# Two attention-and-MLP layers on one core: low halves and b2 sums that go to GpSimd or VectorE as the plan finds room, and unit 1's residual on ScalarE

## The chip, the cores and the metric

The kernel runs on one core of one Trainium2 chip. The metric is device time in microseconds. Three runs of the kernel before gave 1146.32, 1146.71 and 1148.91, with a median of 1146.71.

## What is computed

The input x has 2048 rows of 640 numbers. The reference runs two layers; each one is an attention block and then an MLP block, with the same weights in both layers.

```
x = x + attention(layernorm(x), wqkv) @ wo
x = x + gelu(layernorm(x) @ w1 + b1) @ w2 + b2      # w1: 640 x 1536
# and the same two lines once more
```

The attention has 32 heads of 20 numbers. A query looks at eight keys: its own row and the rows 2, 4, ... 14 before it. So a logit is a sum over 20 products, and there are eight of them for a query and a head. The result is compared in float32 accuracy, which is why every matrix operand is split: a high half in float16 and a low half, the float16 of what the high half left out. A product of two split operands takes three matmuls (high by high, high by low, low by high).

## The kernel before: units, groups and a plan

The even and the odd rows are each cut into two sets of 512 (the attention reaches back in steps of two), and a set in one layer is a *unit*: units 0 to 3 are layer 1, units 4 to 7 are layer 2. A unit has four tiles of 128 rows. For a unit n the work is this.

- `layernorm` makes the normalised rows, the high half on ScalarE (line 615) and the low half on VectorE (line 617); a DMA transposes both for the next matmul.
- `qkv` multiplies by wqkv on TensorE (line 874; in units 5 to 7 a form with seven products instead of eight, line 802, whose extra sums and low halves are in `sums_of_rows`, lines 643 to 678). The result goes to DRAM and comes back by query and key (DMAs `qk`, `v`).
- `attention` runs on VectorE, once for each of four groups of eight heads: G = 4n to 4n+3. It multiplies queries by keys (line 965, 5120 elements a partition), sums over the 20 head dimensions (line 970, a reduction of the same 5120 elements), does the softmax on small tiles (lines 974 to 984, the exponential on ScalarE), multiplies by the values (line 986) and adds the eight keys up (lines 991 and 994). Line 999 takes the high half on ScalarE and line 1002 the low half.
- `project` multiplies by wo on TensorE (line 1027) after a transposing DMA (line 1015) of all four groups' halves. The residual is added in one of two ways. In seven units ScalarE first puts x into the PSUM bank (line 1039), the matmuls add to it, and ScalarE copies the sum back (line 1044). In unit 1 (`filled = n != 1`) VectorE adds bank and x instead (line 1036, two instructions of 320 elements a tile, eight in all).
- `mlp` goes over twelve slabs of 128 hidden columns. For each one TensorE makes the hidden values (line 1094, fifteen matmuls), ScalarE applies gelu and takes the high half (lines 1100, 1103), VectorE takes the low half (line 1105), and TensorE multiplies by w2 into five PSUM banks (line 1115; 24 matmuls a slab, the last third of which reads the low half). Units 6 and 7 of the MLP are done together at the end by `pair` and `joint` (lines 1170 to 1420), in a scheme with fewer products.
- b2 is added to x by GpSimd (line 624), once a tile.

No order is written by hand. Each step is handed to a `Plan` with an engine, a duration, a priority, the things it needs and the buffers it holds. `Plan.run` plays the program through once on the host, engine by engine, takes for each engine the ready step that can start first (with the priority to decide between near ones), and the instructions are then issued in the order of their planned starts. So the table of durations and priorities sets the order on every engine, and a change in one rule moves instructions everywhere.

GpSimd has a rule of its own. VectorE's steps with two operands in SBUF are marked as a pair (`PAIRS`), and a step on GpSimd marked so is not planned to start inside one of them; if it takes over 1 us in the plan, it also waits on the chip for the VectorE instruction that stands before it in the plan (`behind`), and VectorE's next pair step is planned after its end. Two kinds use this: the low half of the first three attention groups of a unit (line 1002, `ol` in the plan, planned at 1.7 us) and the sums with b2 (line 624, `xb`). The fourth group's low half is on VectorE.

## Time and profile before

| | us |
|---|---|
| median of three runs | 1146.71 |
| the profiled execution, whole | 1149.85 |
| its span, first to last instruction | 1148.1 |
| TensorE (PE) busy | 1125.1 |
| VectorE (DVE) busy | 1072.3 |
| ScalarE (ACT) busy | 630.2 |
| GpSimd (POOL) busy | 144.4 |
| mean granted TensorE clock | 0.999 |

The profiled execution is 1.75 us longer than its span, which holds what lies before the first and after the last instruction, and 3.14 us longer than the median. Lines of the profile give an engine, the source line, what is written and read, and how often. A matmul's duration in the profile reaches into the next one, so its cost is taken as a group's busy time over its count. PEclk is the clock that TensorE was granted, as a share of full speed.

### The profile page before, as it was taken

How to read it: one execution, taken by the hardware profiler on the slowest of the kernel's cores; microseconds unless marked ns; L12 is line 12 of the kernel's file. 1: busy time of each engine (PE TensorE's matmuls, PEld its weight loads, DVE VectorE, ACT ScalarE, POOL GpSimd, SP SyncE). 2: the span in 40 equal slices, each digit the busy share in tenths (PEclk: the TensorE clock that was granted, in tenths of full speed). 3: DMA queues.
4: the chain of work that ended last, by engine and by line, in shares of the span. 5: the costliest groups of instructions: out<-in, count | busy, mean ns of one | idle time of the engine just before them, and what ended most of it. 6: DMA issues, size and time to landing. Idle time of an engine off the chain costs nothing.

```text
span 1148.1 us, 16909 instructions
## 1 busy us (share of the span) xinstructions
PE 1125.1 (98%) x6560; PEld 604.1 (53%) x6560; DVE 1072.3 (93%) x901; ACT 630.2 (55%) x1163; POOL 144.4 (13%) x94
## 2 busy tenths in 40 slices
PE   9999999999999999999999999999999999989998
PEld 6444445445544465455555464456444655544476
DVE  7999999999999999999999999999999999498972
ACT  6367327343863373555567664388634852776630
POOL 1012014100041101100021002111220120010000
PEclk9999999999999999999999999999999999999999
DMA  9998784768787799568956879768878574896101
GB/s 320 304 299 256 206 197 143 206 219 252 219 279 199 219 283 285 190 240 213 323 163 217 196 220 298 226 195 185 231 252 242 215 192 139 215 219 178 45 24 69
DMA packets 257564, 246.05 MB, mean 214 GB/s; under 512 B 150524, under 2 KB 215116, under 8 KB 257484
## 3 DMA queue, kind: packets, MB, share of 16 engines
q1 hardware_dynamic: 257484, 244.98, 73.9%
q8 instruction: 51, 0.84, 0.3%
q14 instruction: 29, 0.24, 0.1%
HBM read 157.55 MB, written 52.64 MB: 183 GB/s over the span
## 4 chain that ended last, share of the span: by engine, by line
PE 32%; DVE 19%; issue 6%; ACT 5%; DMA 2%; POOL 1%; POOLq 0%; SPq 0%; DVEq 0%; ACTq 0%
PE ps L1094 8%; PE acc L1115 8%; PE ps L802 6%; PE ps L1027 4%; DVE pr L965 3%; PE acc L1296 3%; DVE sm L970 3%; DVE pr L991 2%; PE ps L1296 2%; DVE pr L986 2%; DVE pr L1228 2%; PE ps L1331 1%; DVE wq L736 1%; DMA wq<-ws0T 1%; DVE act L1105 1%
## 5 line engine op out<-in xcount | busy, mean ns | idle before, releaser
L1115 PE MATMUL acc<-c,act 128*128 128x512 f16 (+1 forms) x1728 | 249.0, 299 | 3.6 <-DVE xf L1159 2.0
L874 PE MATMUL ps<-wq,yT 128*128 128x480 f16 (+1 forms) x1230 | 244.4, 361 | 0.4 <-DVE yT L536 0.2
L1094 PE MATMUL ps<-yT,c 128*128 128x512 f16 x1080 | 243.1, 379 | 1.0 <-DMA yT<-w 1.0
L1115 PEld LDWEIGHTS <-act 128*128 128x128 f16 x1728 | 136.2, 98 | 113.2 <-issue 3.3
L874 PEld LDWEIGHTS <-yT 128*128 128x128 f16 x1230 | 118.9, 98 | 124.6 <-ACT yT L534 0.5
L965 DVE TENSOR_TENSOR pr<-qk 128x5120 f32<-128x5120 f32 x32 | 176.6, 5519 | 1.0 <-DMA qk<-spill 0.7
L986 DVE TENSOR_TENSOR pr<-sm,v 128x5120 f32<-128x5120 f32 x32 | 176.5, 5516 | 0.4
L970 DVE TENSOR_REDUCE sm<-pr 128x256 f32<-128x5120 f32 x32 | 175.1, 5472 | 0.1
L1094 PEld LDWEIGHTS <-c 128*128 128x128 f16 x1080 | 103.6, 98 | 122.2 <-issue 1.1
L991 DVE TENSOR_TENSOR pr<-pr 128x2560 f32<-128x2560 f32 x64 | 142.0, 2219 | 0.4
L1027 PE MATMUL ps<-wo,yT 128*128 128x320 f16 x960 | 134.4, 301 | 4.4 <-DMA yT<-ohl 2.6
L1027 PEld LDWEIGHTS <-yT 128*128 128x128 f16 x960 | 94.2, 98 | 43.7 <-DMA yT<-ohl 3.6
L1100 ACT ACTIVATE act<-ps,b 128x512 f32<-128x512 f32 x72 | 49.1, 682 | 106.2 <-PE ps L1094 105.5
L584 POOL TENSOR_TENSOR ln<-ln,half 128x2 f32<-128x2 f32 (+1 forms) x31 | 48.7, 1574 | 410.7 <-ACT ln L581 410.7
L1002 POOL TENSOR_TENSOR ohl<-w,ohl 128x640 f16<-128x640 f32 x24 | 49.2, 2049 | 401.1 <-DVE pr L965 202.2
L892 ACT ACTIVATE ev<-ps 128x480 f32<-128x480 f32 x80 | 45.1, 567 | 99.1 <-PE ps L874 94.9
L802 PE MATMUL ps<-wq,yT 128*128 128x480 f16 x396 | 84.3, 366 | 0.0
L811 ACT ACTIVATE ev<-ps 128x480 f32<-128x480 f32 x72 | 39.5, 565 | 49.3 <-PE ps L802 44.6
L802 PEld LDWEIGHTS <-yT 128*128 128x128 f16 x396 | 38.2, 98 | 40.0
L802 PE MATMUL ps<-wq 128*128 128x480 f16 x252 | 53.8, 366 | 2.9 <-ACT ev L811 2.1
L567 ACT ACTIVATE junk<-xf 128x640 f16<-128x640 f32 x57 | 41.7, 731 | 19.4 <-DVE xf L1036 11.7
L1105 DVE TENSOR_TENSOR act<-act 128x512 f16<-128x512 f32 x72 | 51.0, 716 | 1.0 <-ACT act L1103 0.8
(218 smaller groups left out, 1247.3 us busy)
## 6 DMA issues: line engine op xcount, KB each, us to landing
c<-mw SPq DMA_DIRECT2D x126, 320.0 KB, 3.8
spill<-ev SPq DMA_DIRECT2D x64, 480.0 KB, 4.3
qk<-spill SPq DMA_DIRECT2D x32, 880.0 KB, 6.1
v<-spill SPq DMA_DIRECT2D x32, 880.0 KB, 5.2
qk<-spill SPq DMA_DIRECT2D x32, 320.0 KB, 3.1
c<-in_B_w_dram SPq DMA_DIRECT2D x24, 320.0 KB, 4.8
mw<-c SPq DMA_DIRECT2D x24, 320.0 KB, 3.7
pr<-in_B_w_dram SPq DMA_DIRECT2D x24, 320.0 KB, 3.4
```

Source lines behind the costliest of these rows:

```text
L802: nc.tensor.matmul(ps, r(x_, j), w[:, j, y_], start=start and i == 0, stop=i == len(todo) - 1, skip_group_check=True)
L874: nc.tensor.matmul(ps, transposed(yk)[:, a * KD + k, t * P:(t + 1) * P], wq[:, g, k, b, i0 * GC:i1 * GC], start=first and j == 0, stop=las ...
L965: nc.vector.tensor_mul(pr.rearrange("p w t c -> p w (t c)"), w[:, HALO + m:HALO + 2 * m].rearrange("p t c -> p (t c)")[:, None, :].to_broa ...
L970: dve(E, G - 0.7, lambda: nc.vector.tensor_reduce(by_key(), heads(), axis=AX.X, op=OP.add), need=[("qk", G)], give=[("lg", G)], use=[*pk, sk])
L986: dve(E, G - 0.85, lambda: nc.vector.tensor_mul(heads(), by_key()[:, :, :, None].to_broadcast([P, W, m * GH, DH]), windows(tile_of(*vw), [ ...
L991: dve(m * w * GC, G - 0.9, lambda w=w: nc.vector.tensor_add(pr[:, 0:w], pr[:, 0:w], pr[:, w:2 * w]), need=[last], give=[("ad", G, w)], use=vk)
L1002: eng.tensor_sub(tile_of(*hk)[:, :, 1, g * GC:(g + 1) * GC], ot(), hi())
L1027: nc.tensor.matmul(tile_of(*pk)[:, :D // 2], transposed(yk)[:, a * KD + k, t * P:(t + 1) * P], wo[:, b, k, c * D // 2:(c + 1) * D // 2], s ...
L1094: nc.tensor.matmul(tile_of(*pk)[:, :nt], tile_of(*ck)[:, a, k * P:(k + 1) * P], transposed(yk)[:, c * KD + k, t0 * P:t1 * P], start=i == 0 ...
L1105: dve(nt, -1000, lambda h32=h32, hk=hk: nc.vector.tensor_sub(tile_of(*hk)[:, 1, :nt], tile_of(*h32)[:, :nt], tile_of(*hk)[:, 0, :nt]), nee ...
L1115: nc.tensor.matmul(accs[k][:, c0:c0 + n], tile_of(*hk)[:, a, (i - t0) * P:(i - t0 + 1) * P], tile_of(*wk)[:, c, w0:w0 + n], start=first, s ...
L1296: nc.tensor.matmul(tile_of(*to(i))[:, :HALF], hl()[:, a, i * P:(i + 1) * P], row(c), start=start and (a, c) == PASS[0], stop=(a, c) == PAS ...
```

## The change

Five kinds of step lose their fixed engine. They are handed to the plan as VectorE's, with a second duration for GpSimd (`aside`), and the plan keeps each in the ready lists of both engines and gives it to the one that can start it first:

- `hlo`, the low half of the MLP's hidden values (72, all on VectorE before)
- `yl`, the low half of the normalised rows (44) and of the seven-product form's sums of rows (24), all on VectorE before
- `ol`, the low half of the attention's output (32; 24 on GpSimd and 8 on VectorE before)
- `xb`, the sum with b2 (24, all on GpSimd before)

Two rules bind them. On GpSimd such a step may only start after the begin of VectorE's latest sum over head dimensions (line 970 before, 1003 after; `lg` in the plan) and must end, as planned, at most 0.2 us after that sum (`OVER`). On VectorE it sorts as if it became ready only `HOLD` microseconds later: 2 for `hlo`, 12 for `yl` of an attention layernorm and for `ol` of the first three groups, 50 for `xb`, 0 for the others.

Apart from that, unit 1's residual takes the way of the other units (`filled = True`), and unit 4's qkv is told to stand behind unit 3's (`behind`). Lines after the table move down by 29 to 33: 617 becomes 648, 624 becomes 654, 970 becomes 1003, 994 becomes 1027, 1002 becomes 1035, 1027 becomes 1056, 1105 becomes 1134, 1115 becomes 1144, 1331 becomes 1360.

```diff
+HOLD = {'s': 0.0, 'hlo': 2.0, 'a': 12.0, 'b': 0.0, 'xb': 50.0, 'ol': 12.0, 'ol3': 0.0}
...
+    OVER = 0.2
...
+        def arrives(o):
+            o["born"] = now
+            ready.setdefault(o["eng"], []).append(o)
+            if o["aside"]:
+                ready.setdefault("pool", []).append(o)
...
-            if o["pair"] and o["eng"] == "pool":
+            if o["aside"] and by == "pool":
+                if not open_:
+                    return None
+                t = max(t, open_[-1][0] + 0.1)
+                if t + o["aside"] > open_[-1][1] + self.OVER:
+                    return None
+            elif o["pair"] and by == "pool":
...
-                    key = (max(t - o["wait"], clock[e] + 0.05), o["prio"], o["n"])
+                    key = (max(t - o["wait"], clock[e] + 0.05, (o["born"] + o["hold"]) * (e == "dve")), o["prio"], o["n"])
...
+                if kind == "lg":
+                    open_.append((t, t + d))
...
+    def either(n, hold, prio, emit, need=(), give=(), use=(), aside=None):
+        dve(n, prio, emit, need, give, use, aside=aside or 0.12 + n / 500.0, hold=hold)
...
-            dve(D, first(t), lambda key=key, parts=parts: nc.vector.tensor_sub(parts()[:, 1], tile_of(*key), parts()[:, 0]),
+            either(D, HOLD['b' if twice else 'a'], first(t), lambda eng, key=key, parts=parts: eng.tensor_sub(parts()[:, 1], tile_of(*key), parts()[:, 0]),
...
-                pool(ASIDE, -200 + n, lambda t=t: nc.gpsimd.tensor_add(x[u][:, t], x[u][:, t], b2),
-                     need=[("y", name, t), ("qk", G), "b2"], give=[("xb", n, t)], pair=True)
+                either(D, HOLD['xb'], 100 + n, lambda eng, t=t: eng.tensor_add(x[u][:, t], x[u][:, t], b2),
+                       need=[("y", name, t), "b2"], give=[("xb", n, t)], aside=1.6)
...
-        if at < NG - 1:
-            pool(ASIDE, -300 + G, lambda: lo(nc.gpsimd), need=[("oh", G), ("qk", G + 1)], give=[("ol", G)], use=[ok, hk],
-                 pair=True)
-        else:
-            dve(m * GC, -300 + G, lambda: lo(nc.vector), need=[("oh", G)], give=[("ol", G)], use=[ok, hk])
+        either(m * GC, HOLD['ol'] if at < NG - 1 else HOLD['ol3'], -300 + G, lo, need=[("oh", G)], give=[("ol", G)], use=[ok, hk])
...
-        filled = n != 1
+        filled = True
...
-            dve(nt, -1000, lambda h32=h32, hk=hk: nc.vector.tensor_sub(
+            either(nt, HOLD['hlo'], -1000, lambda eng, h32=h32, hk=hk: eng.tensor_sub(
```

The program's order shows what the plan made of it. The first place is the end of GpSimd's list. Before, it holds low halves of the attention (L1002, `ohl` from a work tile `w`), sums with b2 (L624, `xf`) and the power of a layernorm's variance (L584, `ln`).

```order
L584 TENSOR_TENSOR ln_90<-ln_90,half 128x2
L624 TENSOR_TENSOR xf<-xf,b_104 128x640 x2
L1002 TENSOR_TENSOR ohl_75<-w_83,ohl_75 128x4x160
L624 TENSOR_TENSOR xf<-xf,b_104 128x640 x2
L1002 TENSOR_TENSOR ohl_75<-w_82,ohl_75 128x4x160
L584 TENSOR_TENSOR ln_91<-ln_91,half 128x2
L1002 TENSOR_TENSOR ohl_75<-w_85,ohl_75 128x4x160
```

After, the same place also has the MLP's low halves (L1134, `act`) and a low half of the sums of rows (L708, `w`).

```order
L1035 TENSOR_TENSOR ohl_75<-w_82,ohl_75 128x4x160
L615 TENSOR_TENSOR ln_90<-ln_90,half 128x2
L708 TENSOR_TENSOR w_86<-w_85,w_86 128x640
L1134 TENSOR_TENSOR act<-act 128x512
L615 TENSOR_TENSOR ln_91<-ln_91,half 128x2 x2
L1134 TENSOR_TENSOR act<-act 128x512
L1035 TENSOR_TENSOR ohl_75<-w_82,ohl_75 128x4x160
L1134 TENSOR_TENSOR act<-act 128x512
```

Over the whole list GpSimd has 17 `ol`, 17 `xb`, 13 `hlo`, 12 `yl` and 4 low halves of sums of rows where it had 24 `ol` and 24 `xb`: 63 long instructions for 48. VectorE loses those 13, 12 and 4 and the eight residuals, and gains 7 `ol` and 7 `xb`.

The second place is VectorE around the last sum of unit 0's attention (the second L994 of the rows, into `w_86`), whose low half (L1002) is the last thing that unit 0's projection needs. Before:

```order
L994 TENSOR_TENSOR w_85<-pr 128x640
L986 TENSOR_TENSOR pr<-sm_88,v_68 128x5120
L991 TENSOR_TENSOR pr<-pr 128x2560
L991 TENSOR_TENSOR pr<-pr 128x1280
L994 TENSOR_TENSOR w_86<-pr 128x640
L965 TENSOR_TENSOR pr<-qk_67 128x5120
L1002 TENSOR_TENSOR ohl_75<-w_86,ohl_75 128x4x160
L970 TENSOR_REDUCE sm_87<-pr 128x8x32
```

And after, where L1019 and L1024 are the product with the values and the sums over keys, L1027 is the last sum, L998 the next group's product of queries and keys, and L648 is `yl`:

```order
L648 TENSOR_TENSOR w_85<-w_86,w_85 128x640
L1024 TENSOR_TENSOR pr<-pr 128x2560
L1024 TENSOR_TENSOR pr<-pr 128x1280
L1035 TENSOR_TENSOR ohl_75<-w_82,ohl_75 128x4x160
L1027 TENSOR_TENSOR w_82<-pr 128x640
L998 TENSOR_TENSOR pr<-qk_67 128x5120
L1035 TENSOR_TENSOR ohl_75<-w_82,ohl_75 128x4x160
L648 TENSOR_TENSOR w_84<-w_83,w_84 128x640
L1003 TENSOR_REDUCE sm_87<-pr 128x8x32
```

The fourth group's low half still stands behind a product of 5120 elements. Ahead of the sum, VectorE has eight `yl` fewer than before and one `ol` more. On TensorE unit 0's projection stands 30 matmuls of qkv (line 874) earlier than before.

The third place is TensorE behind the last projection, unit 7's. Before, the first products of the closing pair (L1331, weights `c`) follow it at once:

```order
L1027 LDWEIGHTS yT_72
L1027 MATMUL ps_92<-wo,yT_72 128x320
L1331 LDWEIGHTS c_76
L1331 MATMUL ps_93<-yT_74,c_76 128x512
```

After, the last slab of the last single MLP (L1144) comes behind the projection:

```order
L1056 LDWEIGHTS yT_74
L1056 MATMUL ps_93<-wo,yT_74 128x320
L1144 LDWEIGHTS act
L1144 MATMUL acc_96<-c_81,act 128x512
L1144 LDWEIGHTS act
L1144 MATMUL acc_100<-c_81,act 128x128
```

72 matmuls of that MLP, which stood ahead of the projection, now stand behind it: 24 at once, and the other 48 in between the first six, nine, six, nine and six products of the pair. The number of TensorE's rows is the same in both programs (13,090), and so are its kinds of matmul.

## Prediction before the run

> **What bounds the kernel now.** I read the page first, then the busy time of each engine by stage, then who waits for whom on TensorE, and last the groups of VectorE and GpSimd. The page's head says that TensorE is all but full and VectorE nearly so.
>
> ```profile
> span 1148.1 us, 16909 instructions
> PE 1125.1 (98%) x6560; PEld 604.1 (53%) x6560; DVE 1072.3 (93%) x901; ACT 630.2 (55%) x1163; POOL 144.4 (13%) x94
> ```
>
> The change leaves TensorE's matmuls as they are, so what it can win is TensorE's idle time, 1148.1 - 1125.1 = 23.0 us, and time in which its clock was low. The busy time by stage (columns: stretch, its length, then PE, PEld, DVE, ACT, POOL busy, granted clock, DMA) tells where that lies:
>
> ```profile
> 0.00:155.00 155.00, 153.23 (x830) 79.31 (x831) 143.38 (x127) 81.29 (x156) 20.15 (x23) 1.00 0.90 269
> 155.00:180.00 25.00, 22.42 (x136) 13.58 (x134) 24.61 (x13) 12.38 (x30) 0.56 (x1) 0.93 0.81 191
> 180.00:480.00 300.00, 296.55 (x1711) 155.21 (x1709) 292.69 (x207) 149.80 (x270) 51.46 (x29) 1.00 0.78 233
> 480.00:975.00 495.00, 490.85 (x2901) 260.44 (x2901) 490.36 (x347) 294.11 (x551) 67.74 (x39) 1.00 0.76 218
> 975.00:1005.00 30.00, 28.36 (x193) 17.74 (x191) 13.92 (x29) 22.42 (x47) 0.69 (x1) 1.00 0.87 217
> 1005.00:1075.00 70.00, 63.97 (x322) 31.21 (x321) 64.46 (x105) 49.81 (x78) 3.78 (x1) 1.00 0.70 178
> 1075.00:1148.10 73.10, 69.68 (x479) 46.62 (x477) 42.90 (x79) 20.36 (x34) 0.00 (x0) 1.00 0.11 39
> ```
>
> TensorE's idle time by stage is length less busy: 1.8, 2.6, 3.5, 4.2, 1.6, 6.0 and 3.4. The first is the start and the last the end of the program, where the change moves nothing that TensorE waits for. In the stage of unit 0's projection the clock was low as well:
>
> ```profile
> 164.00:168.00 4.00, 2.87 (x15) 1.76 (x16) 4.00 (x2) 0.36 (x1) 0.00 (x0) 0.76 1.18 242
> 168.00:172.00 4.00, 4.00 (x26) 2.63 (x25) 4.00 (x3) 1.76 (x4) 0.00 (x0) 0.81 1.04 315
> ```
>
> Worked out from these, 2.87 x 0.24 + 4.00 x 0.19 = 1.5 us were lost there behind the wait of 2.6. What the waits end on (engine, what waited, what released it: us in total, times, longest):
>
> ```profile
> PE ps L1027 <- DMA yT<-ohl: 2.6, 1, 2.6
> PE ps L802 <- ACT ev L811: 2.1, 2, 1.7
> PE acc L1115 <- DVE xf L1159: 2.0, 2, 1.2
> PE ps L1331 <- ACT ev L1352: 1.7, 1, 1.7
> PE ps L1027 <- ACT ps L1039: 1.6, 1, 1.6
> PE acc L1296 <- ACT act L1303: 1.1, 1, 1.1
> PE ps L1094 <- DMA yT<-w: 1.0, 1, 1.0
> PE acc L1115 <- DVE act L1105: 0.8, 1, 0.8
> PE acc L1115 <- DVE c L470: 0.8, 1, 0.8
> ```
>
> No wait is long. Most stand behind a VectorE that is 98 to 99% busy from 180 to 975 (292.69 of 300, 490.36 of 495): the transposed low halves (`ohl`, `w`), a low half of the MLP, a low half of a weight. Those of L1331 and L1296 are in the closing pair, where a product waits for ScalarE's copy of the one before. So two engines are in balance, and relief for VectorE is worth at most the waits behind it.
>
> **What the change takes off VectorE.** The groups that it touches (mean ns behind the busy time), and the reduction beside which GpSimd is now to work:
>
> ```profile
> L970 DVE TENSOR_REDUCE sm<-pr 128x256 f32<-128x5120 f32 x32 | 175.1, 5472 | 0.1
> L1105 DVE TENSOR_TENSOR act<-act 128x512 f16<-128x512 f32 x72 | 51.0, 716 | 1.0 <-ACT act L1103 0.8
> L617 DVE TENSOR_TENSOR w<-w,w 128x640 f16<-128x640 f32 x44 | 36.8, 854 | 6.0 <-ACT w L615 6.0
> L1002 DVE TENSOR_TENSOR ohl<-w,ohl 128x640 f16<-128x640 f32 x8 | 6.5, 818 | 1.3 <-ACT ohl L999 1.3
> L1036 DVE SCALAR_TENSOR_TENSOR xf<-ps,xf 128x320 f32<-128x320 f32 x8 | 3.5, 482 | 0.5 <-PE ps L1027 0.4
> L1002 POOL TENSOR_TENSOR ohl<-w,ohl 128x640 f16<-128x640 f32 x24 | 49.2, 2049 | 401.1 <-DVE pr L965 202.2 <-DVE pr L986 148.7 <-ACT ps L820 15.5
> ```
>
> By the counts of the order, VectorE loses 13 `hlo` (13 x 0.716 = 9.3), 12 `yl` and 4 low halves of row sums (16 x 0.854 = 13.7) and 8 residuals (8 x 0.482 = 3.9), and gains 7 `ol` and 7 `xb` (14 x 0.818 = 11.5, `xb` taken like the 640 elements of `ol`). The sum is -15.4 us of 1072.3. L617 also stood idle for 6.0 us, waiting for ScalarE's high half. With a hold of 12 us or on GpSimd a part of that goes.
>
> Then there is what GpSimd does to VectorE. This is a run of GpSimd beside the reduction, which takes its usual time, and GpSimd takes 1.40 us for a low half and 3.06 for two sums with b2:
>
> ```profile
> 338.89 5.48 DVE L970 TENSOR_REDUCE sm<-pr 128x256 f32<-128x5120 f32 x1
> 339.12 1.40 POOL L1002 TENSOR_TENSOR ohl<-w,ohl 128x640 f16<-128x640 f32 x1 [0.20 <-DVE act L1105]
> 340.48 3.06 POOL L624 TENSOR_TENSOR xf<-xf,b 128x640 f32<-128x640 f32 x2
> ```
>
> And these are meetings with a two-operand instruction:
>
> ```profile
> 83.70 6.57 DVE L986 TENSOR_TENSOR pr<-sm,v 128x5120 f32<-128x5120 f32 x1
> 321.94 3.90 POOL L1002 TENSOR_TENSOR ohl<-w,ohl 128x640 f16<-128x640 f32 x1 [20.16 <-DVE pr L986]
> 324.50 2.02 DVE L470 SCALAR_TENSOR_TENSOR c<-c,c 128x640 f16<-128x640 f32 x1
> 811.16 6.66 POOL L624 TENSOR_TENSOR xf<-xf,b 128x640 f32<-128x640 f32 x1 [0.77 <-DVE sm L978]
> 965.34 2.49 DVE L1105 TENSOR_TENSOR act<-act 128x512 f16<-128x512 f32 x2
> ```
>
> One side waits for the whole of the other: GpSimd's 1.4 us become 3.90 or 6.66, then VectorE's 0.82 become 2.02. VectorE has thirteen instructions that are 1.1 to 1.35 us longer than their equals in this way, the first at 83.70 and the last at 965.34, some 15.4 us together. The page "SBUF — State Buffer" of the Trainium skill (section "Who interferes with whom") has it as a rule: a two-input VectorE instruction and a GpSimd one that reads SBUF exclude each other for a whole instruction, a reduction never does. The trace agrees, by the rows above.
>
> The change plans GpSimd's 63 long instructions inside reductions alone, where 48 had more places. I take a third of the thirteen meetings to remain (0 to all of them), so some 10 us more come off. VectorE then has 15 to 37 us less to do, and I count on 25.
>
> **What TensorE gets from it, stage by stage.** TensorE's costs by group, busy over count, are 0.199 us (L874), 0.144 (L1115) and 0.225 (L1094):
>
> ```profile
> L1115 PE MATMUL acc<-c,act 128*128 128x512 f16 (+1 forms) x1728 | 249.0, 299 | 3.6 <-DVE xf L1159 2.0
> L874 PE MATMUL ps<-wq,yT 128*128 128x480 f16 (+1 forms) x1230 | 244.4, 361 | 0.4 <-DVE yT L536 0.2
> L1094 PE MATMUL ps<-yT,c 128*128 128x512 f16 x1080 | 243.1, 379 | 1.0 <-DMA yT<-w 1.0
> ```
>
> *Unit 0's projection* (2.6 + 1.5 = 4.1 before). TensorE reaches it 30 x 0.199 = 6.0 us earlier. VectorE reaches the last sum 8 x 0.854 - 0.818 = 6.0 earlier, so the wait stays, less the meeting at 83.70 and ScalarE's part in L617's waits. I take 2.0 in all, 1.3 of wait and 0.7 of clock, from 0 to 5.6. By the Trainium skill's page "TensorE: Matmul & The Clock Gate" (section "Part 1: The HAM clock gate") the clock falls only after an idle window of about 3.4 us. Here 2.6 us came before it; by the rule the wait alone could be won, and the whole gain would be about 0.8 us less.
>
> *180 to 480* (3.5). A low half of a weight behind the meeting at 324.50 (0.8), an MLP low half behind a reduction (0.8, now open to GpSimd) and a late transpose (1.0) have lost their cause. New waits will come with a new order. I take 2.0, from 0.5 to 7.
>
> *480 to 975* (4.2). The waits of L802 and L1115 are for ScalarE's copies and VectorE's drains, which only gain by VectorE's relief. I take 3.0, from 1 to 10.
>
> *Unit 7's projection* (1.6). TensorE reaches it 72 x 0.144 = 10.4 us earlier. Ahead of VectorE's last sum are 15 `hlo`, 16 `yl` and row sums and 8 residuals less and 14 others more: 10.7 + 13.7 + 3.9 - 11.5 = 16.8 us, and the meetings besides. I take 0.3, from 0 to 2.
>
> *The closing pair* (6.0). The 72 matmuls now stand between its first products, so that the copies of ScalarE (1.7 and 1.1 in the waits) run beside 10.4 us of other work. The later waits stay. I take 3.0, from 1.5 to 6.
>
> ScalarE pays: 16 copies of 320 elements for unit 1 and eight more table loads by the order.
>
> ```profile
> L1039 ACT ACTIVATE ps<-xf 128x320 f32<-128x320 f32 x56 | 23.6, 432 | 0.4
> L1100 ACT ACT_TABLE_LOAD x19 | 24.4, 1283 | 0.3
> ```
>
> 16 x 0.432 + 8 x 1.283 = 17.2 us on an engine that is at half load in every stage but the pair. In seven units TensorE keeps pace with the copies, so I cost them at nothing. If that cover is gone, a table load in the softmax's way costs 1.3 us a time. Moving unit 4's qkv behind unit 3's I also cost at nothing, since it only fixes an order between full matmul runs.
>
> The new wait is on GpSimd: each long instruction waits for the VectorE instruction ahead of its reduction. Queued behind it are the layernorm powers, for which ScalarE waits, and other low halves.
>
> The sum: before 1.8 + 4.1 + 3.5 + 4.2 + 1.6 + 6.0 + 3.4 = 24.6; after 1.8 + 2.0 + 2.0 + 3.0 + 0.3 + 3.0 + 3.4 = 15.5. That is -9.1, so the profiled execution's 1149.85 would be 1140.8, and the median, 3.1 below it, 1137.6. Low ends alone give 8.2, or -16.4 (1130.3). High ends give 35.8 and a loss of 11 us (1158).
>
> **The rivals.**
>
> *No change: the waits move to other projections.* TensorE comes to unit 1's projection 75 x 0.199 - 15 x 0.225 - 6 x 0.144 = 10.7 us earlier, and VectorE has hardly less ahead of it: 7 `yl` less, but 3 `ol`, one `hlo` and two weight halves more, some -1. If 3.5 us of waiting come up there, units 0's 4.1 stay and the middle stages keep 3.5 and 4.2, the sum is 1.8 + 4.1 + 3.5 + 3.5 + 4.2 + 0.3 + 3.0 + 3.4 = 23.8 for 24.6, or 1145.9. For it speaks that TensorE's new order runs ahead at units 0, 1 and 4; against it, that VectorE also loses meetings and waits.
>
> *Slower: an MLP low half that misses its reduction.* The thirteen `hlo` on GpSimd are the one kind that TensorE needs at once. If VectorE and ScalarE run a few us apart from the plan, one stands behind a product as the sum with b2 at 811.16 does, 6.7 us. Between its high-half and low-half matmuls TensorE has fifteen matmuls of L1094, 3.4 us, so a miss costs 3.3. Two or three eat the gain, and from four on the kernel is slower. With five it is 1137.6 + 16.5 = 1154. Against it: the planned order waits on VectorE's own progress, and the run at 339.12 lies inside its reduction with an end to spare.
>
> *Much slower: the port is never free.* "Perfetto Trace Analysis" of the Trainium skill (section "Optimizing Scalar/DVE Operations") warns that moving work between VectorE and GpSimd might not help, since they share a read port. As a mechanism here: if all 63 instructions held VectorE up by 1.2 us, that is 75.6 for 15.4 now, less the 15.4 of work taken away, +45 on an engine at 99%, so about 1190. The reduction of 5.48 us beside three GpSimd instructions speaks against it.
>
> **How the numbers follow.** A measurement of this kernel can tell about 0.2%, 2.3 us, from no change: 1144.4 to 1149.0 is the same. My forecast, 1137.6, with its own range 1130.3 to 1144, gets 0.69; no change 0.13, of which a little falls below 1144.4; the missed low halves 0.15; the port 0.03. Faster is then 0.71, same 0.12, slower 0.17. The range 1130 to 1150 leaves out most of the last two rivals and the far end of the forecast, about 0.2.
>
> **What would show it.** Right: VectorE's busy time down by some 25 us, few stretched instructions, low halves on GpSimd of 1.1 to 1.4 us beside L1003, unit 7's projection beginning some 16 us earlier (10.4 of order and what the waits ahead of it lose), and TensorE's idle time near 15 us with the pair's first waits gone. Wrong: `PE acc L1144` waiting for `POOL act L1134`, GpSimd instructions of 3 to 7 us, or waits of several us at `PE ps L1056` for `DMA yT<-ohl`.

## The result and the profile after

The changed kernel takes 1137.07 us (the median of four runs, 1136.49 to 1137.40). The kernel before, run beside it, takes 1147.45. The ratio is 0.9908, with a 95% interval from 0.9891 to 0.9925. So it is faster by 0.92%, or 10.4 us.

The page's head, after:

```profile
span 1135.6 us, 16918 instructions
PE 1121.8 (99%) x6560; PEld 603.4 (53%) x6560; DVE 1043.6 (92%) x878; ACT 648.4 (57%) x1187; POOL 149.9 (13%) x109
```

VectorE's busy time fell by 28.7 us (from 1072.3), and ScalarE's rose by 18.2. TensorE's idle time (span less busy) fell from 23.0 to 13.8. The busy time by stage, with the later stages moved to where the same work now stands (columns as before):

```profile
0.00:155.00 155.00, 152.14 (x825) 78.70 (x826) 144.18 (x124) 81.23 (x156) 28.19 (x29) 1.00 0.90 273
155.00:180.00 25.00, 25.00 (x165) 15.94 (x164) 24.07 (x18) 19.33 (x50) 4.71 (x4) 1.00 0.73 179
180.00:480.00 300.00, 299.80 (x1736) 156.62 (x1735) 298.31 (x202) 166.09 (x299) 46.07 (x32) 1.00 0.78 238
480.00:965.00 485.00, 480.31 (x2825) 254.62 (x2824) 458.07 (x331) 290.98 (x529) 68.07 (x43) 1.00 0.77 221
965.00:995.00 30.00, 29.81 (x208) 18.68 (x207) 22.43 (x43) 26.40 (x53) 2.90 (x2) 1.00 0.67 164
995.00:1065.00 70.00, 67.56 (x348) 33.78 (x347) 55.76 (x88) 45.01 (x71) 0.00 (x0) 1.00 0.67 186
1065.00:1135.60 70.60, 67.20 (x463) 45.09 (x461) 40.83 (x78) 19.32 (x34) 0.00 (x0) 1.00 0.11 38
```

Between 155 and 480 TensorE now stands still for 0.2 us in all, although VectorE is even fuller there than it was (298.31 of 300 from 180 on, for 292.69). In 480 to 965 VectorE is no longer full: 458.07 of 485, where it was 490.36 of 495. TensorE, busy for 480.31 of these 485 us, bounds the kernel there. These are the longest of the waits that TensorE has left (total, times, longest):

```profile
PE ps L1056 <- ACT ps L1068: 1.9, 2, 1.1
PE ps L832 <- ACT ps L850: 1.8, 1, 1.8
PE acc L1325 <- ACT act L1332: 1.4, 1, 1.4
PE acc L1521 <- POOL ident L472: 1.4, 1, 1.4
PE ps L904 <- ACT wq L500: 1.1, 1, 1.1
```

None of these five is for VectorE or for a transposed low half. The groups behind it (mean ns behind the busy time):

```profile
L1003 DVE TENSOR_REDUCE sm<-pr 128x256 f32<-128x5120 f32 x32 | 175.2, 5476 | 0.1
L1134 DVE TENSOR_TENSOR act<-act 128x512 f16<-128x512 f32 x59 | 40.1, 685 | 2.0 <-ACT act L1132 2.0
L648 DVE TENSOR_TENSOR w<-w,w 128x640 f16<-128x640 f32 x32 | 25.9, 819 | 2.0 <-ACT w L646 2.0
L615 POOL TENSOR_TENSOR ln<-ln,half 128x2 f32<-128x2 f32 x26 | 52.4, 2016 | 320.3 <-ACT ln L612 320.3
L654 POOL TENSOR_TENSOR xf<-xf,b 128x640 f32<-128x640 f32 x17 | 26.1, 1546 | 46.6 <-DVE act L1134 30.5 <-PE acc L1144 13.0 <-ACT w L640 3.1
L1035 POOL TENSOR_TENSOR ohl<-w,ohl 128x640 f16<-128x640 f32 x17 | 23.8, 1403 | 204.5 <-DVE sm L1015 45.3 <-DVE sm L1016 40.5 <-DVE act L1134 29.5
L1134 POOL TENSOR_TENSOR act<-act 128x512 f16<-128x512 f32 x13 | 15.1, 1160 | 168.5 <-ACT act L1132 105.6 <-DVE w L708 23.2 <-DVE sm L1017 22.6
```

GpSimd's low half of the attention takes 1403 ns in the mean, where it took 2049, and its sum with b2 1546 for 1758. The reduction keeps its length (5476 ns for 5472). Here three GpSimd instructions lie inside one reduction:

```profile
904.21 5.49 DVE L1003 TENSOR_REDUCE sm<-pr 128x256 f32<-128x5120 f32 x1
904.35 1.16 POOL L1134 TENSOR_TENSOR act<-act 128x512 f16<-128x512 f32 x1 [17.02 <-ACT acc L1104]
905.47 1.41 POOL L1035 TENSOR_TENSOR ohl<-w,ohl 128x640 f16<-128x640 f32 x1
907.63 1.16 POOL L1134 TENSOR_TENSOR act<-act 128x512 f16<-128x512 f32 x1 [0.75 <-ACT act L1132]
```

Of GpSimd's 63 long instructions 62 lie so, and one ends 0.13 us after its reduction. Of VectorE's instructions that are over 0.3 us longer than the median of their form ("stretched", below) the trace before has 14, with 15.7 us together beyond those medians. The trace after has none.

### The profile page after: what moved, and what is told of

It reads as the page before. It is cut to its first block, busy times and chain, and to the rows that moved or that the text cites. A ratio compares the mean times of both kernels' runs of the same rounds, so it can differ in the third digit from the quotient of the medians.

```text
span 1135.6 us, 16918 instructions
## 1 busy us (share of the span) xinstructions
PE 1121.8 (99%) x6560; PEld 603.4 (53%) x6560; DVE 1043.6 (92%) x878; ACT 648.4 (57%) x1187; POOL 149.9 (13%) x109
## 4 chain that ended last, share of the span: by engine, by line
PE 67%; DVE 21%; issue 5%; DMA 4%; ACT 2%; SPq 0%; POOLq 0%; POOL 0%; DVEq 0%; ACTq 0%
PE ps L904 20%; PE ps L1123 14%; PE acc L1144 12%; PE ps L1056 8%; PE ps L832 6%; DVE sm L1003 4%; DVE pr L1019 4%; PE acc L1325 3%; DVE pr L998 3%; PE ps L1360 2%; PE ps L1325 2%; DVE pr L1024 2%; DVE pr L1257 1%; DVE w L708 1%; DMA yT<-w 1%
## 5 line engine op out<-in xcount | busy, mean ns | idle before, releaser
L1144 PE MATMUL acc<-c,act 128*128 128x512 f16 (+1 forms) x1728 | 248.9, 299 | 0.2
L904 PE MATMUL ps<-wq,yT 128*128 128x480 f16 (+1 forms) x1230 | 245.6, 361 | 1.5 <-ACT wq L500 1.1
L1144 PEld LDWEIGHTS <-act 128*128 128x128 f16 x1728 | 135.9, 98 | 110.0 <-issue 0.4
L904 PEld LDWEIGHTS <-yT 128*128 128x128 f16 x1230 | 118.7, 98 | 124.9 <-issue 1.3
L1019 DVE TENSOR_TENSOR pr<-sm,v 128x5120 f32<-128x5120 f32 x32 | 175.5, 5485 | 0.4
L998 DVE TENSOR_TENSOR pr<-qk 128x5120 f32<-128x5120 f32 x32 | 175.5, 5483 | 0.4
L1003 DVE TENSOR_REDUCE sm<-pr 128x256 f32<-128x5120 f32 x32 | 175.2, 5476 | 0.1
L1024 DVE TENSOR_TENSOR pr<-pr 128x2560 f32<-128x2560 f32 x64 | 137.6, 2150 | 0.2
L1056 PE MATMUL ps<-wo,yT 128*128 128x320 f16 x960 | 131.9, 299 | 1.9 <-ACT ps L1068 1.9
L1056 PEld LDWEIGHTS <-yT 128*128 128x128 f16 x960 | 93.8, 98 | 39.6 <-issue 1.6
L615 POOL TENSOR_TENSOR ln<-ln,half 128x2 f32<-128x2 f32 (+1 forms) x31 | 57.9, 1869 | 346.1 <-ACT ln L612 346.1
L832 PE MATMUL ps<-wq,yT 128*128 128x480 f16 x396 | 85.1, 366 | 2.0 <-ACT ps L850 1.8
L832 PEld LDWEIGHTS <-yT 128*128 128x128 f16 x396 | 38.2, 98 | 43.0 <-issue 2.7
L832 PE MATMUL ps<-wq 128*128 128x480 f16 x252 | 54.5, 366 | 0.8 <-ACT ev L841 0.8
L1035 POOL TENSOR_TENSOR ohl<-w,ohl 128x640 f16<-128x640 f32 x17 | 23.8, 1403 | 204.5 <-DVE sm L1015 45.3
L602 ACT ACTIVATE junk<-xf,ln 128x640 f16<-128x640 f32 x57 | 46.8, 820 | 0.5
L1132 ACT ACTIVATE act<-act 128x512 f16<-128x512 f32 x72 | 45.1, 626 | 1.4
```

The lines of the kernel that those rows point to most:

```text
L615: pool(0.5, prio, lambda t0=t0, t1=t1: nc.gpsimd.tensor_tensor(col(2)[:, t0:t1], col(2)[:, t0:t1], half[:, t0:t1], op=OP.pow), need=[("vr" ...
L832: nc.tensor.matmul(ps, r(x_, j), w[:, j, y_], start=start and i == 0, stop=i == len(todo) - 1, skip_group_check=True)
L904: nc.tensor.matmul(ps, transposed(yk)[:, a * KD + k, t * P:(t + 1) * P], wq[:, g, k, b, i0 * GC:i1 * GC], start=first and j == 0, stop=las ...
L998: nc.vector.tensor_mul(pr.rearrange("p w t c -> p w (t c)"), w[:, HALO + m:HALO + 2 * m].rearrange("p t c -> p (t c)")[:, None, :].to_broa ...
L1003: dve(E, G - 0.7, lambda: nc.vector.tensor_reduce(by_key(), heads(), axis=AX.X, op=OP.add), need=[("qk", G)], give=[("lg", G)], use=[*pk, sk])
L1019: dve(E, G - 0.85, lambda: nc.vector.tensor_mul(heads(), by_key()[:, :, :, None].to_broadcast([P, W, m * GH, DH]), windows(tile_of(*vw), [ ...
```

## The experiments

The theory was that VectorE's relief, less work and no meetings, makes the gain, and that the order in which the plan puts things matters little. Rivals: the residual makes it, or the one order does. All twelve kernels compute the whole reference. Each line of the table has the median, the ratio to the kernel before in runs beside it with its interval (before had medians of 1147.97, 1146.80 and 1147.45 us in three sets of runs, each on another chip, so kernels of different sets are best compared by their ratios), and from the profiled run VectorE's busy time, its stretched instructions, TensorE's idle time (span less busy), and how often its clock was halved for 3.41 us before the kernel's end, by the trace's clock records.

| kernel | us | ratio [95%] | VectorE | stretched | idle | halved |
|---|---|---|---|---|---|---|
| before | 1147.45 | 1 | 1072.3 | 14 (15.7 us) | 23.0 | 1 |
| after | 1137.07 | 0.9908 [0.9891, 0.9925] | 1043.6 | 0 | 13.8 | 0 |
| residual alone | 1145.59 | 0.9976 [0.9965, 0.9987] | 1067.4 | 13 (13.9) | 20.1 | 0 |
| no residual | 1148.00 | 0.9994 [0.9984, 1.0005] | 1045.4 | 1 (0.3) | 22.9 | 2 |
| two kinds only | 1144.80 | 0.9968 [0.9952, 0.9985] | 1058.5 | 0 | 20.6 | 1 |
| no window | 1191.76 | 1.0382 [1.0368, 1.0396] | 1064.2 | 66 (61.3) | 53.6 | 10 |
| residual, order kept | 1144.20 | 0.9970 [0.9960, 0.9981] | 1048.0 | 1 (1.2) | 17.7 | 1 |
| all on VectorE, order kept | 1175.35 | 1.0243 [1.0228, 1.0259] | 1087.6 | 0 | 39.2 | 8 |
| no waiting, order kept | 1159.17 | 1.0104 [1.0090, 1.0118] | 1068.3 | 22 (24.7) | 28.5 | 4 |
| hold 3 | 1135.49 | 0.9902 [0.9885, 0.9918] | 1049.2 | 0 | 11.6 | 0 |
| no residual, hold 1 | 1137.04 | 0.9909 [0.9896, 0.9922] | 1046.4 | 0 | 13.8 | 0 |
| no residual, hold 3 | 1156.56 | 1.0084 [1.0061, 1.0107] | 1048.0 | 1 (0.5) | 28.2 | 4 |
| hold 14 | 1141.81 | 0.9953 [0.9941, 0.9965] | 1045.6 | 0 | 16.4 | 1 |
| low halves only | 1152.59 | 1.0046 [1.0034, 1.0059] | 1056.1 | 22 (24.8) | 23.9 | 4 |

### The parts of the change

*Residual alone*: the kernel before with one line changed.

```diff
-        filled = n != 1
+        filled = True
```

> The kernel before with one edit: unit 1's residual goes through ScalarE (filled = True). GpSimd keeps its 24 low halves and 24 b2 sums where they were. Theory W (the gain is VectorE's relief, and most of it is that GpSimd works inside the reductions and no longer meets two-operand instructions): VectorE loses 8 x 0.482 = 3.9 us and keeps some 13 meetings, so 1143 to 1147. Rival R (the residual carries the change): 1140 or less. Rival O (any new plan shuffles the waits; which part does it is chance): anything from 1137 to 1150.

It gave 1145.59, 2.4 us less than before. VectorE's meetings with GpSimd stay (13 stretched instructions for 14).

*No residual*: the changed kernel with that line put back.

```diff
-        filled = True
+        filled = n != 1
```

> The changed kernel without the residual's edit (filled = n != 1). By the order GpSimd has 64 long instructions, all planned inside reductions. Theory W: VectorE has 3.9 us more work than with the change and still no meetings, so 1137 to 1141, at most three stretched VectorE instructions. Rival R: the gain is gone, 1144 or more.

It gave 1148.00: the whole gain is gone, although VectorE has as little to do as after (1045.4 us) and meets GpSimd once. The theory of relief failed here. The trace shows VectorE standing still for some 30 us where it had work in the other kernels (start, length, and the idle time ahead in brackets):

```profile
841.57 0.82 DVE L654 TENSOR_TENSOR xf<-xf,b 128x640 f32<-128x640 f32 x1
854.64 1.16 DVE L864 TENSOR_TENSOR ev<-ev,ev 128x960 f32<-128x960 f32 x1 [12.25 <-ACT ev L841]
869.26 0.83 DVE L648 TENSOR_TENSOR w<-w,w 128x640 f16<-128x640 f32 x1 [13.47 <-ACT w L646]
874.13 5.49 DVE L998 TENSOR_TENSOR pr<-qk 128x5120 f32<-128x5120 f32 x1 [4.04 <-DMA qk<-spill]
```

L864 and L998 belong to unit 7's qkv and to the attention that it feeds. On TensorE this kernel runs unit 6's projection (L1056) among unit 7's qkv (L832):

```profile
846.51 6.28 PE L1056 MATMUL ps<-wo,yT 128*128 128x320 f16 x45
...
859.73 6.28 PE L1056 MATMUL ps<-wo,yT 128*128 128x320 f16 x45
865.85 5.02 PE L832 MATMUL ps<-wq,yT 128*128 128x480 f16 x24
...
889.55 3.62 PE L832 MATMUL ps<-wq,yT 128*128 128x480 f16 x9 [2.41 <-ACT ev L841]
```

In the changed kernel that qkv is done before the projection begins:

```profile
855.19 1.99 PE L832 MATMUL ps<-wq,yT 128*128 128x480 f16 x9
857.01 3.42 PE L1144 MATMUL acc<-c,act 128*128 128x512 f16 x24
860.27 3.40 PE L1123 MATMUL ps<-yT,c 128*128 128x512 f16 x15
864.05 16.46 PE L1056 MATMUL ps<-wo,yT 128*128 128x320 f16 x120
```

The bill comes at unit 7's projection, at 980 us of the run without the residual:

```profile
PE ps L1056 <- ACT ps L1068: 7.5, 2, 5.7
```

What is late there is VectorE's last low half of the attention, which that projection needs through a transposing DMA. It is done at 977.4 us:

```profile
975.71 1.71 DVE L1035 TENSOR_TENSOR ohl<-w,ohl 128x640 f16<-128x640 f32 x2
```

In the changed kernel it is done at 953.7:

```profile
952.83 0.83 DVE L1035 TENSOR_TENSOR ohl<-w,ohl 128x640 f16<-128x640 f32 x1 [2.16 <-ACT ohl L1032]
```

So a second theory was formed (B in the texts on record): the loss is this order, not the residual.

*Two kinds only*: of the flexible steps just `ol` and `xb` stay flexible; the residual is changed as well.

```diff
+        on = give[0][0] in ("ol", "xb")
-        dve(n, prio, emit, need, give, use, aside=aside or 0.12 + n / 500.0, hold=hold)
+        dve(n, prio, emit if on else lambda: emit(nc.vector), need, give, use, aside=(aside or 0.12 + n / 500.0) if on else None, hold=hold if on else 0.0)
```

> The changed kernel, but only the attention's low halves and the b2 sums may go to either engine; the low halves of the MLP, of the layernorms and of the sums of rows stay on VectorE. By the order GpSimd has 38 long instructions for 48 before. VectorE's own work is then some 10 x 0.82 - 3.9 = 4.3 us more than before, but the 15.4 us of meetings should be gone. Theory W: VectorE is relieved by 11 us in all, 1139 to 1143. Rival L (only the work taken off VectorE counts): no gain or a loss, 1147 to 1150.

It gave 1144.80. All meetings go, VectorE loses 13.8 us, and 2.4 us of TensorE's idle time go with them. Long waits for transposed low halves stay, one of 3.7 us at an MLP's first matmuls and one of 2.5 at unit 0's projection. Freedom for two kinds is enough to end the meetings, and not enough for the gain: the theory's 1139 to 1143 was missed.

*Low halves only*: the other way about. `ol` and `xb` stay fixed as in the kernel before.

```diff
-                either(D, HOLD['xb'], 100 + n, lambda eng, t=t: eng.tensor_add(x[u][:, t], x[u][:, t], b2),
-                       need=[("y", name, t), "b2"], give=[("xb", n, t)], aside=1.6)
+                G = NG * n + (6, 6, 7, 7)[t]
+                pool(ASIDE, -200 + n, lambda t=t: nc.gpsimd.tensor_add(x[u][:, t], x[u][:, t], b2),
+                     need=[("y", name, t), ("qk", G), "b2"], give=[("xb", n, t)], pair=True)
...
-        either(m * GC, HOLD['ol'] if at < NG - 1 else HOLD['ol3'], -300 + G, lo, need=[("oh", G)], give=[("ol", G)], use=[ok, hk])
+        if at < NG - 1:
+            pool(ASIDE, -300 + G, lambda: lo(nc.gpsimd), need=[("oh", G), ("qk", G + 1)], give=[("ol", G)], use=[ok, hk],
+                 pair=True)
+        else:
+            dve(m * GC, -300 + G, lambda: lo(nc.vector), need=[("oh", G)], give=[("ol", G)], use=[ok, hk])
```

> The changed kernel with only the low halves and row sums free to go to either engine; the sums with b2 and the additions of the attention's output stay on GpSimd as in the kernel before, wherever VectorE is. It computes the whole reference. VectorE then issues the least work of all versions (34 of the low halves and row sums on GpSimd beside 48 fixed ones), but the fixed ones may meet its two-operand instructions again. Theory W (what counts is the work taken off VectorE and that no product meets a two-operand instruction): 10 to 16 us of stretched instructions come back, 1139 to 1146 us. Rival L (only the instructions taken off VectorE count): 1137 us or less.

It gave 1152.59, which is over both expectations. Here VectorE's own work is 1031.3 us (1056.1 less 24.8 of stretching), 12.3 less than in the changed kernel, and that does not help. The meetings came back, with more than the 10 to 16 us expected, and one wait is the dearest of the run:

```profile
295.79 2.39 PE L1149 MATMUL acc<-c,act 128*128 128x128 f16 x17
305.25 1.76 PE L1149 MATMUL acc<-c,act 128*128 128x512 f16 x6 [7.07 <-DVE c L501]
```

VectorE does a product of 5.43 us and a reduction of 5.48 us ahead of that low half of a weight. The clock falls within this wait, at 302.07 us, and stays halved behind it:

```profile
302.10:308.90 6.80, 3.65 (x11) 1.45 (x11) 6.80 (x8) 3.02 (x4) 2.32 (x2) 0.50 0.68 226
```

### The rules, with the order kept or not

*No window*: the rule that binds GpSimd to VectorE's reductions is taken out.

```diff
-            if o["aside"] and by == "pool":
-                if not open_:
-                    return None
-                t = max(t, open_[-1][0] + 0.1)
-                if t + o["aside"] > open_[-1][1] + self.OVER:
-                    return None
-            elif o["pair"] and by == "pool":
+            if o["pair"] and by == "pool":
```

> The changed kernel without the window rule: a step given to GpSimd obeys only the old rule (not planned to begin inside a two-operand instruction), as before. By the order GpSimd then has 130 long instructions, 47 of them low halves of the MLP. Theory W: some 80 of them lie outside reductions and meet two-operand instructions at about 1.2 us each, 96 us, against about 55 us of work taken off VectorE; VectorE's busy time is no lower than before, low halves reach TensorE late, and the time is 1150 to 1185. Rival L: VectorE has 55 us less than with the change, so the time is at or below the change's, 1128 to 1137.

It gave 1191.76, +3.8%, over the theory's 1150 to 1185. GpSimd is busy for 316.5 us instead of 149.9. VectorE's own work is 40.7 us less than after, but 61.3 us of stretching come on top:

```profile
PE 1137.3 (95%) x6560; PEld 608.5 (51%) x6560; DVE 1064.2 (89%) x808; ACT 634.2 (53%) x1177; POOL 316.5 (27%) x179
```

*No waiting, order kept*: the changed kernel's order on every engine, but GpSimd's flexible steps no longer wait on the chip for the VectorE instruction ahead of them in the plan.

```diff
-        if "behind" in o:
+        if "behind" in o and not o["aside"]:
```

> The changed kernel with its own order kept, but GpSimd's long instructions no longer wait for the VectorE instruction ahead of their reduction; they start when their operands are there. Theory W (the place beside the reduction is what makes them free): many start early, meet products of 5.5 us, and either stand for up to 5 us or hold VectorE up by 1.2 to 1.4 us each; with 30 to 60 meetings VectorE gets 36 to 75 us longer and the time is 1145 to 1175. Rival (the plan's order of GpSimd's list alone keeps them apart): under 1140.

It gave 1159.17. GpSimd starts too early and meets VectorE's products; its low half takes 4.0 us in the mean for 1.4, and 22 instructions of VectorE are stretched by 24.7 us:

```profile
L1035 POOL TENSOR_TENSOR ohl<-w,ohl 128x640 f16<-128x640 f32 x17 | 68.5, 4027 | 136.4 <-ACT ohl L1032 136.4
```

With the order fixed, this costs 22.1 us of time for 24.7 us of stretching. How much of it is VectorE's lengthening, and how much that GpSimd's own results come later, is not told apart.

*All on VectorE, order kept*: the same order, with the 63 steps issued on VectorE at their places.

```diff
-            o["emit"](nc.gpsimd if o["eng"] == "pool" else nc.vector)
+            o["emit"](nc.vector)
...
-        if "behind" in o:
+        if "behind" in o and not o["aside"]:
```

> The changed kernel with its own order kept, but the 63 instructions that the plan gave to GpSimd are issued on VectorE, at the same places of the order. VectorE's work grows by 13 x 0.68 + 50 x 0.82 = 50 us. Theory W (VectorE's relief is what TensorE's waits fall by): VectorE was idle for about 27 us between 480 and 965 with the change, so some 20 to 30 of the 50 show, 1155 to 1172, and the waits stand at the projections. Rival (TensorE alone bounds the changed kernel and GpSimd's part is spare): under 1145.

It gave 1175.35, over the theory's 1155 to 1172 and 38.3 us more than after for 44.0 us more work on VectorE, without one meeting:

```profile
PE 1135.3 (97%) x6560; PEld 607.4 (52%) x6560; DVE 1087.6 (93%) x941; ACT 645.8 (55%) x1187; POOL 58.3 (5%) x46
```

In this fixed order, then, work on VectorE is paid for almost in full. Part of that time is halved clock (the last section). It is not the price where the plan can be made anew: the kernel before has 63 - 48 = 15 of these steps and the residuals more on VectorE, and the meetings, for 10.4 us.

*Residual, order kept*: unit 1's residual is issued on VectorE at the place where ScalarE's copy stood.

```diff
-                                             wo[:, b, k, c * D // 2:(c + 1) * D // 2], start=not filled and i == 0,
+                                             wo[:, b, k, c * D // 2:(c + 1) * D // 2], start=n == 1 and i == 0,
...
-                    act(D // 2, -700 + n, lambda part=part, pk=pk: nc.scalar.activation(part(), tile_of(*pk)[:, :D // 2], AF.Copy, scale=1.0 / WS),
+                    act(D // 2, -700 + n, lambda part=part, pk=pk, residual=residual: residual() if n == 1 else nc.scalar.activation(part(), tile_of(*pk)[:, :D // 2], AF.Copy, scale=1.0 / WS),
```

> The changed kernel with its own order kept: the plan is made as with the change, but when the instructions are issued, unit 1's residual goes back to VectorE (ScalarE's copies into the bank are left out, and the sum stands on VectorE where ScalarE's copy out stood). So nothing but eight instructions differs. Theory P (the earlier run without the residual lost its gain because its new order starved VectorE of unit 6's and 7's keys, not because of the 3.9 us): 1137 to 1140. Rival R (the residual itself is worth the gain): 1144 or more.

It gave 1144.20, 7.1 us more than after. That is outside theory P's 1137 to 1140 and, for this one run, where rival R put it (1144 or more). The loss is at unit 1's projection and behind it:

```profile
PE ps L1056 <- DVE xf L1065: 2.4, 2, 1.4
PE acc L1144 <- ACT c L500: 1.9, 1, 1.9
```

The first number is for two waits of TensorE for a drain, the step that empties a PSUM bank. On VectorE the drains stand behind a reduction of 5.48 us that began at 261.24 and a product of 5.49 that began at 268.95; on ScalarE they stood behind neither. So in this order, and at these places, the residual is worth more than its 3.9 us of VectorE's time.

### The order

*Hold 3*: the changed kernel with `HOLD` of `hlo` at 3 in place of 2, which makes another plan with 56 long instructions on GpSimd.

```diff
-HOLD = {'s': 0.0, 'hlo': 2.0, 'a': 12.0, 'b': 0.0, 'xb': 50.0, 'ol': 12.0, 'ol3': 0.0}
+HOLD = {'s': 0.0, 'hlo': 3.0, 'a': 12.0, 'b': 0.0, 'xb': 50.0, 'ol': 12.0, 'ol3': 0.0}
```

> The changed kernel with one number of the table moved, the MLP low half's hold from 2.0 to 3.0 us; the same rules, another order (by the order GpSimd has 56 long instructions for 63, unit 7's projection stands at about the same place). Theory W (any order with the window rule and this much relief keeps the gain): 1134 to 1141. Rival O (the size of the gain is this one order's): 1142 or more.

It gave 1135.49. The two intervals overlap almost whole, so it is as good as the changed kernel.

*Hold 14*: the same with the hold `a` of the layernorm's low halves at 14 (the text on record calls it the hold on the scores' side).

```diff
-HOLD = {'s': 0.0, 'hlo': 2.0, 'a': 12.0, 'b': 0.0, 'xb': 50.0, 'ol': 12.0, 'ol3': 0.0}
+HOLD = {'s': 0.0, 'hlo': 2.0, 'a': 14.0, 'b': 0.0, 'xb': 50.0, 'ol': 12.0, 'ol3': 0.0}
```

> The changed kernel with the hold of the products on the scores' side raised to 14 us: another order with 60 products on GpSimd, unit 6's projection behind unit 7's qkv. It computes the whole reference. Theory W (the relief of VectorE beside its reductions makes the gain, and the exact order little): 1134 to 1141 us. Rival O (the gain is luck of the one order): anywhere from 1137 to 1150 us, as likely over 1141 as under.

It gave 1141.81, just over the theory's range. Nearly half of the gain is lost at two places of the order: a wait of 3.1 us at 388 us with a halved clock behind it, and 1.6 at 317.

*No residual, hold 1* and *no residual, hold 3*: the test of B. Both leave unit 1's residual on VectorE; only the hold of `hlo` is different (1.0 and 3.0), and by it the place of unit 6's projection. (The first text on record says raised to 1.0; from the 2.0 of the changed kernel it is lowered.)

```diff
-HOLD = {'s': 0.0, 'hlo': 2.0, 'a': 12.0, 'b': 0.0, 'xb': 50.0, 'ol': 12.0, 'ol3': 0.0}
+HOLD = {'s': 0.0, 'hlo': 1.0, 'a': 12.0, 'b': 0.0, 'xb': 50.0, 'ol': 12.0, 'ol3': 0.0}
...
-        filled = True
+        filled = n != 1
```

> The changed kernel with unit 1's residual back on VectorE and the hold of the hlo products raised to 1.0 us. It computes the whole reference. In its order unit 6's projection stands behind unit 7's three qkv parts (which begin at 812, 832 and 846 us of TensorE's work), as in the changed kernel; in the order without the residual alone it stood among them (848, 865 and 877). Theory B (the loss of the run without the residual is that order, in which VectorE starved for some 30 us between 842 and 874 us, and not the residual): 1136 to 1141 us. Rival R (the residual on ScalarE itself is worth some 10 us): 1144 us or more.

> The changed kernel with unit 1's residual back on VectorE and the hold of the hlo products raised to 3.0 us. It computes the whole reference. Here unit 6's projection stands ahead of unit 7's last qkv parts (848, 865 and 877 us of TensorE's work). Theory B: 1145 to 1150 us, with VectorE idle for over 20 us between 835 and 880 us and TensorE waiting 5 us or more at unit 7's projection. Rival R: 1144 us or more too, but without that idle time of VectorE; the two are told apart by the run beside it.

They gave 1137.04 and 1156.56. The first, without the residual on ScalarE, is as fast as the changed kernel, so rival R is out: the gain does not need that edit. The busy time between 835 and 880 us tells the two orders apart (third group of numbers: VectorE, of 45 us). Hold 1, with unit 7's qkv ahead of the projection:

```profile
835.00:880.00 45.00, 45.00 (x273) 25.74 (x272) 40.77 (x26) 22.65 (x50) 2.31 (x2) 1.00 0.76 250
```

Hold 3, with the projection among it:

```profile
835.00:880.00 45.00, 45.00 (x277) 25.94 (x276) 12.30 (x15) 24.72 (x54) 0.69 (x1) 1.00 0.72 202
```

And the first kernel without the residual:

```profile
835.00:880.00 45.00, 45.00 (x263) 25.54 (x262) 14.73 (x12) 27.80 (x62) 1.39 (x2) 1.00 0.72 208
```

VectorE loses 26 to 28 us there, and what it could have done then is late at unit 7's projection: the last low half is done at 953.9 us with hold 1, and at 984.2 with hold 3. There hold 3 waits for 6.8 us, with two halved clock periods from within the wait on. In the first kernel without the residual the three waits of TensorE behind the starved stretch (2.4, 5.7 and 1.8 us) and two halved periods of 1.7 us each make 13.3 us, and its span is 13.5 longer than that of hold 1. VectorE's share of the stretch is not all, though: hold 14 has it busy for 29.71 us there and does not wait at unit 7's projection. That the time came out 6.6 us over B's range is not the branch alone: 2.0 and 2.4 us of further waits at 591 and 611 us and 2.1 at 318, two of them with a halved clock, are places of this plan's own.

## Why the prediction was right

The forecast for the median, 1137.6, is 0.5 us from the 1137.07 measured. Two errors cancel in that. The profiled execution was put at 1140.8 and took 1137.4, so the sum was 3.4 us short of the gain. And the 3.1 us by which the profiled execution before stood above its median were taken off after as well, where it stands only 0.3 above. The sum, term by term (TensorE's idle time in us, in unit 0's row with what the low clock lost):

| stage | before | forecast | after |
|---|---|---|---|
| start | 1.8 | 1.8 | 2.9 |
| unit 0's projection | 4.1 | 2.0 | 0.0 |
| up to 480 | 3.5 | 2.0 | 0.2 |
| up to unit 7's projection | 4.2 | 3.0 | 4.7 |
| unit 7's projection | 1.6 | 0.3 | 0.2 |
| closing pair | 6.0 | 3.0 | 2.4 |
| end | 3.4 | 3.4 | 3.4 |
| sum | 24.6 | 15.5 | 13.8 |

That is -10.8 for -9.1. The span fell by 12.5; the other 1.7 lie in TensorE's busy time, and no run here tells them apart.

- **VectorE's relief, 25 forecast, 28.7 measured.** The step that was mis-sized is the third of the meetings that was to remain. None did (15.7 us of stretching to 0), since each GpSimd step waits for the instruction ahead of its reduction. The work taken off was then 28.7 - 15.7 = 13.0 for 15.4. Part of that gap is that the means used, 0.716 and 0.854, held meetings; without them they are 0.685 and 0.819.
- **Unit 0's projection and up to 480, 4.0 forecast, 0.2 measured.** "The wait stays" failed: unit 0's projection now begins at 157.37 us, 7.8 earlier than before, and without a wait. TensorE comes to it 5.2 us earlier (6.0 forecast) and VectorE to the last low half 8.8 us earlier (146.36 for 155.14 us; 6.0 forecast), so it was there in time. How much of that is the meeting at 83.70 and how much L617's waits is not told apart. And "new waits will come with a new order" did not hold in this stretch.
- **From 480 on, 3.0 forecast, 4.7 measured.** All of the 4.7 us are waits for ScalarE; before, 2.1 of that stretch's waits were. So the part for VectorE's drains and DMAs went, as forecast, and the part for ScalarE's copies, which was only to gain, more than doubled.
- **The start, said to be untouched, lost 1.1 us.** A wait of L904 for a half of a weight on ScalarE is new.
- **Unit 7's projection and the pair.** The projection begins at 964.28 for 982.23, 18.0 us earlier where some 16 were forecast, and its 1.6 us of waiting are gone; the 0.2 left in the row is a wait of the pair. The pair's first wait (1.7) is gone, as told; the one for a high half on ScalarE (1.1), which was to be covered too, stays with 1.4.
- **ScalarE, costed at nothing, 17.2 us forecast, 18.2 measured.** TensorE waits for two of ScalarE's fills of a bank with x, 1.9 us in all, both at unit 3's projection (515 and 531 us), where it was one and 1.6. So ScalarE was not free of cost everywhere; whether the added copies and table loads make the waits from 480 on, no run tells.
- **The rivals.** The waits did not move to unit 1's projection: TensorE comes to it 15.1 us earlier (259.44 for 274.52) and does not wait there. No MLP low half missed its reduction: the 13 on GpSimd take 1160 ns in the mean, and L1144 does not wait for GpSimd. The port was free, by the same means and the reduction's 5476 ns. The Trainium skill's page "SBUF — State Buffer" (section "Who interferes with whom"), that a reduction never shares the lock, agrees with the 62 that lie wholly inside one; the Trainium skill's page "Perfetto Trace Analysis" (section "Optimizing Scalar/DVE Operations"), that such moves might not help, is what happens without the window (66 stretched instructions, +3.8%).

What the prediction did not see is how far the order alone carries. It took the relief to be worth its waits in any order that the plan would make, with 1130 to 1150 for all that. Five more kernels of the table have plans of their own and the same relief, VectorE at 1045 to 1049 us with at most one stretched instruction. They took 1135.5, 1137.0, 1141.8, 1148.0 and 1156.6 us. So what is shown is this: the meetings are gone, VectorE has less work, and in the order of the changed kernel that relief is needed, some 0.9 us of time for one of VectorE's (22.1 for 24.7, 38.3 for 44.0). It is not enough by itself: in the two plans in which VectorE is idle for two thirds of the stretch from 835 to 880 us or more, the gain is gone. The prediction did not ask whether the new plan would feed VectorE there; that it does (38.08 us busy of 45) is luck. Whether another plan of the kernel before, without the relief, would give as much was tried only with the residual alone (-0.24%), and stays open, and with it how the 10.4 us divide between relief and order. So does what in the plan's rules throws unit 6's projection to one side or the other.

## What to carry to other kernels

In this kernel work for GpSimd cost VectorE nothing where it lay inside a reduction and waited there for VectorE's real progress (5476 ns a reduction for 5472). Put beside two-operand instructions it cost VectorE more than it took off (61.3 us for 40.7 without the window) and made GpSimd's own instructions longer (4.0 us for 1.4). Where a planner makes the order, one change of a rule redraws it everywhere: run a few neighbouring settings before believing a gain or a loss of a per cent, and look for the stretch where the second engine starves, long before the wait that it causes. A part that seems to carry the gain when it is undone alone (the residual, 10.9 us) may only throw the plan into another order when it is taken away.

## What the hardware showed besides

The clock does not sag, it halves. Here it is in the trace before, behind the wait of 2.6 us at unit 0's projection:

```profile
166.10:169.50 3.40, 3.40 (x15) 1.91 (x13) 3.40 (x3) 0.88 (x2) 0.00 (x0) 0.50 1.11 255
```

The clock records of all fourteen traces hold only full and half clock, and a half-clock period before the kernel's end lasts 3.41 us or twice that, so each costs up to 1.7 us beside its wait (half of 3.41, an estimate). Of TensorE's waits of 3.0 us and more inside the kernels, all but one (3.28) had one about them. Of those from 1.9 to 2.7 some had (among them 1.93 with 0.43 behind it, 2.04, 2.11, 2.31, 2.61) and some had not (among them 2.13, 2.38, 2.47); none below 1.9 had. That the clock is judged over a window of about 3.4 us which runs on by itself is what the Trainium skill's page "TensorE: Matmul & The Clock Gate" states (section "Part 1: The HAM clock gate"). The 3.41 us agree, but a wait far shorter than the window (1.93 us) is enough here. What the prediction worked out by that rule, 0.8 us less of gain, does not hold: by the row above the clock did fall for the 2.6 us. With this, idle time and halved periods add up: the kernel with all on VectorE, order kept, has 39.2 - 13.8 = 25.4 us more idle time and 8 x 1.7 = 13.6 of clock than after, 39.0 together, and its span is 38.9 longer.

A GpSimd instruction of two columns can be long too. The layernorm powers (L615) take 2016 ns in the mean for 1523 before, one of them 5.69 us at 281.69, beside a product of VectorE of 5.48 us that began at 281.34. They are not bound to reductions, and no wait of TensorE after the change is put down to them.
